# Attention stages spaced three slots apart, and one more batch by the seven-product scheme, in an attention and mixture-of-experts kernel

## The chip, the cores and the metric

The kernel runs on one core of a Trainium2 chip. The metric is the device time of one execution in microseconds (us); smaller is better. The kernel before takes 452.4 us (median of three runs, 452.1 to 457.5). The profile is of one execution; its span, from the first to the last instruction, is 450.9 us.

## What is computed

A block of cross attention between a sequence `x` (8 batches, 8 heads, 512 rows, width 64) and a small state (32 rows per head) goes in both directions; its rows then go through a top-1 mixture of eight experts.

```python
scores = x @ state.T * scale;  a  = softmax(scores);   xread = a @ state     # 512 rows per head
scores2 = state @ x.T * scale; a2 = softmax(scores2);  sread = a2 @ x        # 32 rows per head
tok = concat([xread, sread], axis=2) -> 8 * 544 tokens of width 512
e = argmax(tok @ w_gate);  gate = softmax(tok @ w_gate)[e]
out[tok] = gate * (relu(tok @ w1[e]) @ w2[e])       # w1[e]: 512 x 1024, w2[e]: 1024 x 512, float32
```

## The kernel before

The kernel treats the 512 `xread` rows of a batch as one group that goes to the expert which most of them choose (rows that choose another are handled by a branch at the end). It never forms `xread`, but multiplies the states into the expert's first matrix (`G = state @ w1`, in `states_w1`), and then works with the attention weights `a` (in the code `aT[b]`) directly. For each batch there are then two big products on the tensor engine (PE): `up`, `hT = relu(G.T @ aT)`, into PSUM tiles `ph`; and `down`, `hT.T @ w2`, into tiles `py`. The 32 state rows of each head go later through the experts in three *rounds* (tiles `pgh`, `pgy`), whose weights are loaded from DRAM again (tiles `s`).

PE works through the batches' products one after the other. All other work is cut into pieces, Python generators, that are put between the products' matmuls: each `next(insert)` is one *slot*, and emits the next pieces. Every engine works through its instructions in the order in which they were emitted, and each batch's attention passes through the slots as a pipeline of stages:

```python
def stages(b):                       # one batch's attention, before the change
    xt, sx = new_xt(), new_sx()
    turn_x(b, xt, slice(0, 4)); turn_x(b, xt, slice(4, 8))   # DVE: xt <- x_nat (two transposes)
    turn_states(b, gp.tensor_copy)                           # DVE stT, then POOL copies stT, stG
    yield
    states_gates(b)                  # PE pg <- stT;  ACT gst <- pg
    pc = new_pc()                    # the one PSUM tile of four banks for scores
    scores(b, xt, pc, 0)             # PE pc
    yield
    scores(b, xt, pc, 1)
    for i in range(4):
        turn_scores(pc, sx, i)       # DVE sx <- pc
    less_max(sx, ALL, gp)            # DVE mx <- sx, then POOL sx <- sx - mx
    yield
    exponential(sx, ALL)             # ACT sx
    soft[b] = (sx,) + write_weights(pc, write_max(pc))   # DVE nm <- pc, then ACT a <- pc, nm (reads pc)
    over_sum(sx, ALL, gp)            # DVE sm, then POOL sx <- sx * sm
    yield
    turn_read(b)                     # DVE aT <- sx, stored to at_dram by the SP queue
    yield
    yield                            # (an empty stage)
    turn_write(b)                    # PE pt <- a;  ACT a2T <- pt
    yield
    write_rows(b)                    # PE pw; ACT xs <- pw; SP stores srow, then loads x_nat, states of batch b + 3
    exps, gates = logits_x(b)        # PE pl; DVE: the top-1 choice of each row
    yield
    exps(); xsT = turn_rows(b)       # ACT; PE pxs, ACT xsT
    yield
    choose(b); logits_s(b, xsT)      # PE pr; DVE eb: the batch's expert.  PE pls; DVE lgs
    gates()

def first():                         # what is left of batches 0 and 1
    write_rows(0);  yield
    turn_write(1);  yield
    exps, gates = logits_x(1);  yield
    exps(); choose(1); e1 = expert_of(eb, 1)     # the SP queue reads the expert's number
    at_once(w1_parts(1, e1))                     # SP: four loads of w1 for batch 1
    lazy.extend(w2_parts(1, e1)); gates();  yield
    write_rows(1);  yield
    xsT = [turn_rows(b) for b in range(2)];  yield
    for b in range(2): logits_s(b, xsT[b])

def attention():
    gens, slot = [first()], 0
    while gens:
        b = 2 + slot // 4
        new = slot % 4 == 0 and b < B            # a new batch in every fourth slot
        if new:
            gens.append(early.pop() if early else stages(b))
            if b > 2: next(gens[-1])             # its first stage, ahead of the others' in this slot
        for g in gens[:len(gens) - new]: next(g)     # (ends of generators left out)
        slot += 1
        yield

def others():
    yield from attention()
    yield from sort_states()         # the state rows are sorted by expert
    change_pools()                   # attention's tiles are given up; pools for rounds and sums are opened
    yield from rounds(0, NRS)        # NRS = 3
```

The general PSUM tiles (`ph`, `py`, `pG`, `pl`, `pw`, `pt`, `pr`, `pls`, `pg`) share one pool of four banks, `ps_p`. A tile that is asked for waits until an earlier one of the four has been read.

`sort_states` is a chain of small DVE operations from one PE result (`prs`) to the slot of each row. POOL then scatters the rows to DRAM:

```python
    # pr ("prs"): counts by PE; then on DVE ng, cum, ge, eg, gates, base, rk, slot, slot_i, srow, more, own, left ...
    for t in range(NST):             # NST = 2
        gp.indirect_dma_start(out=ss_dram[:], ..., in_=srow[:, t, :])        # POOL
```

Batches below `NE` take the plain products; the others take both by halves, in seven products of half size in place of eight (Strassen's scheme), with operand sums made by DVE and POOL:

```python
def up(G, a, hT, i=ALL, insert=None, every=2, fs=range(NFC)):    # NFC = 8
    for f in fs:
        ph = bank("ph")[:, 0:128 * n]
        for g in range(2): pe.matmul(ph, lhsT=G[:, g, ts(f, 128)], rhs=a[:, i, g, :], ...)
        relu(hT[f // 2][:, f % 2]..., ph...)                     # ACT
        if insert and f % every == every - 1: next(insert, None) # four slots

def down(hT, w2t, store, insert=None, between=None):
    for c in range(NC):                                          # NC = 4
        py = bank("py")
        for f in range(NFC):
            pe.matmul(py[:], lhsT=hT[f // 2][:, f % 2, ts(c, 128)], rhs=w2t[:, f, :], ...)
            if insert and f == 3: next(insert, None)
        store(c, py)                                             # ACT y <- py, and its store
        ...  # between(c): the next batch's G at c == 1 (batch 0: c == 2); then a slot: eight slots in all

def down_by_halves(b, hT, w2t, insert, between):
    Sa, Sb, Ta, Tb = (new_sums(t) for t in ("Sa", "Sb", "Ta", "Tb"))   # in the pools of change_pools
    sums(Sa, ...)                                                # DVE, two adds
    gp.tensor_tensor(Ta[:], W(0, 1), W(0, 0), ALU.subtract)      # POOL
    sums(Sb, ...)                                                # DVE
    gp.tensor_tensor(Tb[:], W(1, 1), W(0, 1), ALU.subtract)      # POOL
    product(pX, A(0, 0), W(0, 0));  ...;  done()                 # done(): a slot; no sums needed
    product(pD, Sa, Ta);  ...;  done()
    ...                                                          # pX again, pY, pZ, pW, pD again: seven slots

def batch(b):
    if b < NE: down(hT, w2s[b], store_batch(b), slots, between)
    else:      down_by_halves(b, hT, w2s[b], slots, between_products)    # also makes the next batch's sums
    if b + 1 in sums_of: hT = up_by_halves(G, aT[b + 1], sums_of[b + 1], new_hT(), slots)   # four slots
    elif b + 1 < B:      hT = up(G, aT[b + 1], new_hT(), insert=slots)

NE = 3
aTl = const.tile([128, B - NE, 4, 2, 128], FP32)      # weights of the batches from NE on; the others' lie in attention's pool
```

`rounds` fetches ahead, and yields empty slots between its pieces:

```python
        round_in(r0); fetch(S1B - 2, S2B)
        for _ in range(4): yield
        for r in range(r0, r1):
            round_x(r); ...; yield
            for k in range(NDC):
                round_up(r, k); fetch(...); yield
                if k < NDC - 1 and r + 1 < r1: yield             # an empty slot, not in the last round
            round_relu(r); yield
            round_h(r); yield
            for f in range(0, NFC, 2):
                ...round_down(r, f + i); fetch(0, 1)...
                if f + 2 == NFC: round_out(r)
                yield
                if r + 1 < r1 or f < 4: yield
```

Of the kernel before, what the change touches and what calls it, by code (L numbers as in the profile page):

```python
# [20 lines left out]
def kernel(  # L21
# [34 lines left out]
    B, H, S, D = x.shape  # L56
# [10 lines left out]
    NDC = DM // 128  # L67
    NFC = F // 128
# [88 lines left out]

    NE = 3  # L160
    aTl = const.tile([128, B - NE, 4, 2, 128], FP32)
    aT = {b: aTl[:, b - NE] for b in range(NE, B)}

# [31 lines left out]
    G = hT = None  # L195
# [45 lines left out]
    def less_max(sx, i, eng):  # L241
        mx = att.tile([128, 4, NB], FP32, tag="mx", bufs=2, name="mx")
        dve.tensor_reduce(mx[:, i], sx[:, i], AX.X, ALU.max)
        eng.tensor_tensor(sx[:, i], sx[:, i], spread(mx, i), ALU.subtract)
# [11 lines left out]
    def write_max(pc):  # L256
        nm = att.tile([128, 2], FP32, tag="nm", bufs=2, name="nm")
        dve.tensor_reduce(nm[:], pc[:, :, 0:256].rearrange("p i (g s) -> p g i s", g=2), AX.XY, ALU.max)
        dve.tensor_scalar(nm[:], nm[:], -SCALE, None, ALU.mult)
        return nm  # L260

    def write_weights(pc, nm):

        a2 = att.tile([128, 2, NC, 128], FP32, tag="a2", name="a2")
        s2 = att.tile([128, 2], FP32, tag="s2", bufs=2, name="s2")
        for g in range(2):
            act.activation(a2[:, g].rearrange("p c (i t) -> p i c t", i=4),
                           pc[:, :, ts(g, 128)].rearrange("p i (c t) -> p i c t", c=NC),
                           AF.Exp, bias=nm[:, g:g + 1], scale=SCALE, accum_out=s2[:, g:g + 1])
        return a2, s2  # L270
# [54 lines left out]
    def logits_x(b):  # L325
        pl = bank("pl")[:, 0:128]
        for g in range(2):
            for i in range(4):
                pe.matmul(pl[ts(i, 32)], lhsT=gst[:, b, g, :], rhs=aT[b][:, i, g, :],
                          start=(g == 0), stop=(g == 1), skip_group_check=True)  # L330
        lg = att.tile([128, NC, 32], FP32, tag="lg", bufs=2, name="lg")
        dve.transpose(lg[:].rearrange("p c e -> p (c e)"), pl)
        return route(lg[:, :, 0:E], b * NC, NC)

    def stages(b):


        xt, sx = new_xt(), new_sx()
        turn_x(b, xt, slice(0, 4))
        turn_x(b, xt, slice(4, 8))  # L340
        turn_states(b, gp.tensor_copy)
        yield
        states_gates(b)
        pc = new_pc()
        scores(b, xt, pc, 0)
        yield
        scores(b, xt, pc, 1)
        for i in range(4):
            turn_scores(pc, sx, i)
        less_max(sx, ALL, gp)  # L350
        yield
        exponential(sx, ALL)
        soft[b] = (sx,) + write_weights(pc, write_max(pc))
        over_sum(sx, ALL, gp)
        yield
        turn_read(b)
        yield
        yield
        turn_write(b)
        yield  # L360
        write_rows(b)
        exps, gates = logits_x(b)
        yield
        exps()
        xsT = turn_rows(b)
        yield
        choose(b)
        logits_s(b, xsT)
        gates()

    def turn_rows(b):

        pt = bank("pxs")
        pe.transpose(pt[:, 0:128], rows_of[b][:].rearrange("p g d -> p (g d)"), ident[:])
        xsT = att.tile([128, 4, NS], FP32, tag="xsT", bufs=2, name="xsT")
        act.copy(xsT[:].rearrange("p q n -> p (q n)"), pt[:, 0:128])
        return xsT
# [208 lines left out]
    def new_hT():  # L586

        return [ffn.tile([128, 2, S], FP32, tag="hT", bufs=NFC // 2, name="hT") for _ in range(NFC // 2)]

    def up(G, a, hT, i=ALL, insert=None, every=2, fs=range(NFC)):  # L590

        n = i.stop - i.start
        for f in fs:
            ph = bank("ph")[:, 0:128 * n]
            for g in range(2):
                pe.matmul(ph, lhsT=G[:, g, ts(f, 128)], rhs=a[:, i, g, :], start=(g == 0), stop=(g == 1))
            relu(hT[f // 2][:, f % 2].rearrange("p (c i t) -> p i c t", c=NC, i=4)[:, i],
                 ph.rearrange("p (i c t) -> p i c t", i=n, c=NC))
            if insert and f % every == every - 1:
                next(insert, None)  # L600
        return hT

# [382 lines left out]
    def rounds(r0, r1):  # L985
        need1.extend((r, k, half) for r in range(r0, r1) for k in range(NDC) for half in range(2))
        need2.extend((r, f) for r in range(r0, r1) for f in range(NFC))
        round_experts(r0)
        fetch(2, 0)
        yield  # L990
        yield
        round_in(r0)
        fetch(S1B - 2, S2B)
        for _ in range(4):
            yield
        for r in range(r0, r1):
            round_x(r)
            if r + 1 < r1:
                round_experts(r + 1)
                round_in(r + 1)  # L1000
            yield
            for k in range(NDC):
                round_up(r, k)
                fetch(2, 2 if r == NRS - 1 and k > 1 else 0)
                yield
                if k < NDC - 1 and r + 1 < r1:
                    yield
            round_relu(r)
            yield
            round_h(r)  # L1010
            yield
            for f in range(0, NFC, 2):
                for i in range(2):
                    round_down(r, f + i)
                    fetch(0, 1)
                if f + 2 == NFC:
                    round_out(r)
                yield
                if r + 1 < r1 or f < 4:
                    yield  # L1020


# [3 lines left out]
    def first():  # L1026

        write_rows(0)
        yield
        turn_write(1)  # L1030
        yield
        exps, gates = logits_x(1)
        yield
        exps()
        choose(1)
        e1 = expert_of(eb, 1)
        at_once(w1_parts(1, e1))
        lazy.extend(w2_parts(1, e1))
        gates()
        yield  # L1040
        write_rows(1)
        yield
        xsT = [turn_rows(b) for b in range(2)]
        yield
        for b in range(2):
            logits_s(b, xsT[b])

    def attention():

        gens, slot = [first()], 0  # L1050
        while gens:
            b = 2 + slot // 4
            new = slot % 4 == 0 and b < B
            if new:
                gens.append(early.pop() if early else stages(b))
                if b > 2:
                    next(gens[-1])
            for g in gens[:len(gens) - new]:
                try:
                    next(g)  # L1060
                except StopIteration:
                    gens.remove(g)
            slot += 1
            yield
# [8 lines left out]
    def batch(b):  # L1073

        nonlocal G, hT

        def between(c):
            nonlocal G
            if c == (1 if b else 2) and b + 1 < B:
                G = states_w1(new_G(), w1s[b + 1], stG[:, b + 1])  # L1080
            yield
            if c == 1 and 0 < b < B - 2:
                lazy.extend(w1_parts(b + 2, expert_of(eb, b + 2)))
            yield

        def between_products(n):
            nonlocal G
            if n in (3, 4) and b + 1 < B:
                if n == 3:
                    G = new_G()  # L1090
                states_w1(G, w1s[b + 1], stG[:, b + 1], (n - 3,),
                          lambda name: late["ps_t"].tile([128, 512], FP32, tag="t", bufs=2, name=name))
            yield
            if n == 4 and b + 2 < B:
                lazy.extend(w1_parts(b + 2, expert_of(eb, b + 2)))
            if n == 5 and b + 1 < B:
                sums_of[b + 1] = up_sums(G, aT[b + 1])
            yield

        if b < NE:  # L1100
            down(hT, w2s[b], store_batch(b), slots, between)
        else:
            down_by_halves(b, hT, w2s[b], slots, between_products)
        if 0 < b < B - 2:
            lazy.extend(w2_parts(b + 2, expert_of(eb, b + 2)))
        if b + 1 in sums_of:
            hT = up_by_halves(G, aT[b + 1], sums_of[b + 1], new_hT(), slots)
        elif b + 1 < B:
            hT = up(G, aT[b + 1], new_hT(), insert=slots)
        if b == 0:  # L1110
            e2 = expert_of(eb, 2)
            lazy.extend(w1_parts(2, e2) + w2_parts(2, e2))
# [127 lines left out]
```

## Time and profile before

| | us |
|---|---|
| time, median of three | 452.4 |
| span of the profiled execution | 450.9 |
| PE busy | 438.8 |
| DVE busy | 199.3 |
| ACT busy | 125.6 |
| POOL busy | 120.3 |

The profile names the engines PE (tensor), PEld (its weight loads), DVE (vector), ACT (scalar), POOL (GpSimd) and SP (the queue that issues most loads). One float32 matmul of the code is two instructions of the trace. A line of the timeline has the start, the duration, the engine, the operation with its tiles, the number of instructions merged, and in brackets how long the engine stood idle before it and what ended the wait. A line of the chain of waits has start, duration and tile.

### The profile page before, as it was taken

To read this page: it belongs to the slowest core of one execution; us is meant where nothing else is said; L and a number is where in the kernel's file an instruction comes from. 1 tells how busy PE (TensorE), PEld (TensorE's weight loads), DVE (VectorE), ACT (ScalarE), POOL (GpSimd) and SP (SyncE) were. 2 spreads that over 40 slices of the span, in tenths; PEclk is the share of its full clock that TensorE was granted. 3 is DMA by queue.
4 is the path that set the end of the run, shared out by engine and by line. 5 is a ranking of instruction groups with operands and counts; after the bars stand their busy time and mean duration, and the time that the engine had idled before them with its cause. 6 is when DMAs were issued, how large, how long until landed. Compare 5 with 4: busy or idle time off the path is not lost.

```text
span 450.9 us, 9945 instructions
## 1 busy us (share of the span) xinstructions
PE 438.8 (97%) x3861; PEld 276.8 (61%) x3861; DVE 199.3 (44%) x452; ACT 125.6 (28%) x283; POOL 120.3 (27%) x108
## 2 busy tenths in 40 slices
PE   8899999999999999999999999999999999999995
PEld 7675545455455455444757776776667776657673
DVE  4758771757383753142241441445143433326142
ACT  1543243434242442313210332024111312024100
POOL 2010140314121211006233413542253423532220
PEclk9999999999999999999999999999999999999998
DMA  6990399324858443519999999799969997498301
GB/s 189 328 312 6 109 322 298 129 87 125 302 146 307 134 161 117 171 49 292 391 383 321 391 388 331 276 354 388 346 217 337 367 405 252 156 365 307 115 26 59
DMA packets 68418, 110.04 MB, mean 244 GB/s; under 512 B 12943, under 2 KB 27279, under 8 KB 68368
## 3 DMA queue, kind: packets, MB, share of 16 engines
q1 hardware_dynamic: 60240, 99.99, 64.2%
q10 hardware_dynamic: 7728, 8.34, 5.2%
q0 software_dynamic: 400, 1.05, 0.6%
q8 instruction: 31, 0.51, 0.5%
q14 instruction: 19, 0.16, 0.1%
HBM read 94.15 MB, written 14.95 MB: 242 GB/s over the span
## 4 chain that ended last, share of the span: by engine, by line
PE 86%; DVE 9%; DMA 2%; issue 1%; POOL 1%; ACT 1%; SPq 0%; POOLq 0%; DVEq 0%
PE ph L48 19%; PE py L48 14%; PE pD L48 8%; PE pX L48 8%; PE pgh L48 5%; PE pgy L48 5%; PE pY L48 4%; PE pW L48 4%; PE pZ L48 4%; PE pc L48 4%; PE pG L48 3%; DVE xt L48 3%; DVE sm L48 2%; PE pw L48 2%; PE pt L48 2%; DMA w1t<-in_moe_w_dram 2%
## 5 line engine op out<-in xcount | busy, mean ns | idle before, releaser
L48 PE MATMUL py<-w2t,hT 128*128 128x512 f32 x192 | 87.6, 601 | 0.0
L48 PEld LDWEIGHTS py<-w2t,hT 128*128 128x128 f32 x192 | 34.6, 190 | 38.7 <-issue 38.0
L48 POOL TENSOR_TENSOR Ta<-w2t,Ta 128x1024 f32<-128x1024 f32 x10 | 26.2, 2621 | 74.5 <-PE pD L48 44.9
L48 PE MATMUL ph<-aTe,G 128*128 128x128 f32 (+2 forms) x160 | 44.9, 430 | 1.2 <-DVE aTe L48 1.1
L48 DVE TENSOR_TENSOR hT<-ph,hT 128x512 f32<-128x512 f32 x40 | 27.7, 692 | 37.4 <-PE ph L48 37.4
L48 ACT ACTIVATE hT<-ph 128x512 f32<-128x512 f32 (+2 forms) x56 | 26.2, 476 | 47.6 <-PE ph L48 47.6
L48 PE MATMUL pX<-w2t,hT 128*128 128x256 f32 x160 | 36.2, 379 | 0.0
L48 PEld LDWEIGHTS ph<-aTe,G 128*128 128x128 f32 x160 | 24.6, 190 | 16.7 <-issue 12.3
L48 PEld LDWEIGHTS pX<-w2t,hT 128*128 128x128 f32 x160 | 30.2, 190 | 4.4 <-issue 0.5
L48 PE MATMUL ph<-aTl,G 128*128 128x256 f32 (+1 forms) x96 | 29.6, 456 | 0.0
L48 POOL TENSOR_TENSOR sx<-sx,mx 128x1024 f32<-128x1024 f32 x6 | 11.5, 1912 | 60.8 <-DVE mx L48 60.8
L48 DVE SCALAR_TENSOR_TENSOR yh<-pY,gw,yh 128x256 f32<-128x256 f32 x20 | 8.3, 476 | 39.6 <-PE pY L48 39.6
L48 PEld LDWEIGHTS ph<-aTl,G 128*128 128x128 f32 x96 | 17.7, 190 | 12.7 <-issue 11.4
L48 ACT ACTIVATE yh<-pX,gw 128x256 f32<-128x256 f32 x30 | 12.0, 473 | 44.8 <-PE pX L48 44.8
L48 ACT COPY G<-pG 128x512 f32<-128x512 f32 x32 | 16.9, 593 | 26.3 <-PE pG L48 26.3
L48 PE MATMUL pgh<-s,sxT 128*32 128x512 f32 x192 | 24.0, 598 | 0.0
L48 PE MATMUL pgy<-s,shT 128*32 128x512 f32 x192 | 23.4, 598 | 0.0
L48 DVE STREAM_TRANSPOSE sx<-pc 128x256 f32<-128x256 f32 x32 | 11.7, 418 | 23.4 <-PE pc L48 23.4
L48 ACT ACTIVATE hT<-hT 128x512 f32<-128x512 f32 x24 | 14.8, 631 | 23.7 <-DVE hT L48 23.7
L48 ACT ACTIVATE y<-py,gw 128x512 f32<-128x512 f32 x12 | 8.2, 687 | 44.1 <-PE py L48 44.1
L48 POOL TENSOR_TENSOR sx<-sx,sm 128x1024 f32<-128x1024 f32 x6 | 11.5, 1914 | 30.7 <-ACT xsT L48 17.0
L48 PE MATMUL pG<-w1t,stG 64*32 64x512 f32 x256 | 18.3, 599 | 0.5 <-DMA w1t<-in_moe_w_dram 0.5
(175 smaller groups left out, 654.8 us busy)
## 6 DMA issues: line engine op xcount, KB each, us to landing
s<-in_moe_w_dram SPq DMA_DIRECT2D x192, 256.0 KB, 5.3
w2t<-in_moe_w_dram SPq DMA_DIRECT2D x32, 512.0 KB, 6.7
w1t<-in_moe_w_dram SPq DMA_DIRECT2D x28, 512.0 KB, 6.0
x_nat<-in_x_dram SPq DMA_DIRECT2D x16, 512.0 KB, 5.4
out_dram<-yh ACTq DMA_DIRECT2D x19, 256.0 KB, 4.9
out_dram<-y ACTq DMA_DIRECT2D x12, 256.0 KB, 2.8
at_dram<-aTl SPq DMA_DIRECT2D x5, 512.0 KB, 5.0
w1t<-in_moe_w_dram SPq DMA_DIRECT2D x2, 1024.0 KB, 7.2
```

The costliest lines, as they stand in the source:

```text
L48: ins = getattr(self.engine, name)(*args, **kw)
```

## The change

Attention is to be over sooner, so that the pools of the seven-product scheme are open one batch earlier. A new batch enters in every third slot instead of every fourth; the stages of a batch go from ten to nine, as one empty stage is dropped; the writing half's maximum and exponentials (`write_max`, `write_weights`) move one stage earlier, next to the scores that they read; `first()` writes batch 1's rows two stages earlier. `up` for batch 2 gives six slots instead of four, so that attention, the sort and the change of pools fit in before batch 2's second product. That product, and batch 3's first, then go by halves (`NE = 2`). The rounds have seven more slots to fill and spread their pieces over them.

```diff
-    NE = 3
+    NE = 2
@@ def stages(b)
     less_max(sx, ALL, gp)
+    soft[b] = (sx,) + write_weights(pc, write_max(pc))
     yield
     exponential(sx, ALL)
-    soft[b] = (sx,) + write_weights(pc, write_max(pc))
     over_sum(sx, ALL, gp)
     yield
     turn_read(b)
-    yield
     yield
     turn_write(b)
@@ def up
-def up(G, a, hT, i=ALL, insert=None, every=2, fs=range(NFC)):
+def up(G, a, hT, i=ALL, insert=None, at=(1, 3, 5, 7), fs=range(NFC)):
-            if insert and f % every == every - 1:
+            if insert and f in at:
@@ def rounds
-        for _ in range(4):
+        for _ in range(7):
             yield
-                if k < NDC - 1 and r + 1 < r1:
+                if k < NDC - 1:
                     yield
-                if r + 1 < r1 or f < 4:
+                if r + 1 < r1 or f + 2 < NFC:
                     yield
@@ def first
     exps, gates = logits_x(1)
+    write_rows(1)
     yield
     (exps, choose(1), the loads of w1 for batch 1)
     gates()
     yield
-    write_rows(1)
-    yield
     xsT = [turn_rows(b) for b in range(2)]
+    yield
     yield
@@ def attention
-            b = 2 + slot // 4
-            new = slot % 4 == 0 and b < B
+            b = 2 + slot // 3
+            new = slot % 3 == 0 and b < B
@@ def batch
-            hT = up(G, aT[b + 1], new_hT(), insert=slots)
+            hT = up(G, aT[b + 1], new_hT(), insert=slots, at=(1, 3, 5, 7) if b + 1 < NE else (1, 3, 4, 5, 6, 7))
+            assert b + 1 < NE or "sst" in late
```

## The prediction

> **What bounds the kernel now.** I read the page first, then busy time by windows of 15 us, then PE's waits, the chain of waits, and the timeline of two stretches. The page:
>
> ```profile
> PE 438.8 (97%) x3861; PEld 276.8 (61%) x3861; DVE 199.3 (44%) x452; ACT 125.6 (28%) x283; POOL 120.3 (27%) x108
> PEclk9999999999999999999999999999999999999998
> ```
>
> PE is the bound, at full clock. A change helps if it takes matmul time away, or one of the few waits, and brings no new wait of PE. The windows (columns: PE, PEld, DVE, ACT, POOL busy, clock, DMA share, GB/s):
>
> ```profile
> 90.00:105.00 15.00, 14.57 (x266) 8.26 (x265) 7.29 (x25) 5.65 (x12) 3.21 (x5) 1.00 0.23 72
> ...
> 210.00:225.00 15.00, 15.00 (x79) 10.85 (x77) 3.97 (x6) 4.62 (x10) 3.38 (x2) 1.00 1.04 380
> ```
>
> In attention PE loses 0.43 us of 15; after it (from 210 us) nothing shows, though DMA is full there. PE's waits say what the 0.43 is (total, times, longest):
>
> ```profile
> PE pg L48 <- POOL stT L48: 2.1, 5, 0.4
> ...
> PE pG L48 <- DMA w1t<-in_moe_w_dram: 0.5, 2, 0.3
> ```
>
> The chain of waits, where it runs through PE, gives the length of each product:
>
> ```profile
> 192.22 7.06 PE py L48 x16
> 199.40 13.84 PE ph L48 x32
> 213.23 3.45 PE pX L48 x16
> 216.69 3.45 PE pD L48 x16
> ...
> 246.04 7.11 PE ph L48 x32
> ...
> 255.00 5.38 PE ph L48 x24
> ...
> 404.45 2.75 PE pgh L48 x16
> ```
>
> At 199.40 stands batch 3's plain up, at 213.23 the start of its down by halves, at 246.04 and 255.00 an up by halves. The pgh of 2.75 us takes 1.85 elsewhere: there it waits for a round's weights.
>
> [...] (below, Ta starts 0.02 us after the scatter ahead of it on POOL, its own data long there). [...] here a subtract of 1024 elements took 2.41 us on POOL (Ta) and 1.22 on DVE (sx). [...] In the trace before, PE's waits hold 0.5 us in all that are put down to ACT (pg after G), so the banks rotate well; the change alters that.
>
> **What the change takes away.**
> - Batch 2's down: eight pieces of 8 matmuls, from the chain 3.63 + 3.44 + 3.63 + 3.44 + 3.63 + 3.43 + 7.06 = 28.3 us. By halves, batch 3's from 213.23 on: 3.45 + 3.45 + 3.46 + 3.65 + 3.65 + 3.65 + 3.45 = 24.8. Gain 3.5.
> - Batch 3's up: 13.84 becomes 7.11 + 5.38 = 12.5. Gain 1.35.
> - The waits of pg: before, DVE does a batch's nm and sm ahead of the next batch's xt and stT. Now xt follows nm directly; from the end of the scores, sx, mx, nm, xt, stT and POOL's copy take 1.5 + 1.2 + 1.4 + 2.3 + 0.7 + 0.7 = 7.8 us, and PE comes to pg after two products and 1.6 us of small matmuls, some 8.8. Gain 2.1.
> - The waits for round weights, 0.9 at 404 and 0.36 at one pgy (2.21 against 1.85): the same loads over 62 slots instead of 55. Gain 1.2.
>
> Sum: 8.2 us. The rest of attention's matmuls (some 5.3 us a batch) is only moved.
>
> **What it adds.** I followed the built program of the changed kernel, which shows each engine's order and for which instruction each wait stands, and laid durations of this trace on it.
>
> (1) The sums behind the sort. Before, batch 3's plain up lay between the sort and the first sums:
>
> ```profile
> 199.21 0.19 PE L48 MATMUL prs<-oh,ones_b 128*128 128x8 bf16 x2
> ...
> 199.43 0.17 DVE L48 TENSOR_SCALAR ng_i<-prs 128x8 int32<-128x8 f32 x1 [5.10 <-PE prs L48]
> ...
> 203.29 1.17 POOL L48 DMA_INDIRECT ss_dram<-srow,slot_i  x1 [30.94 <-DVE more L48]
> 204.76 0.97 POOL L48 DMA_INDIRECT ss_dram<-srow,slot_i  x1 [0.30 <-PE ph L48]
> 205.75 2.41 POOL L48 TENSOR_TENSOR Ta<-w2t 128x1024 f32<-128x1024 f32 x1
> ```
>
> From prs to Ta's end are 208.2 - 199.4 = 8.8 us: 3.9 of small DVE operations, 2.4 of scatters, 2.4 of subtract. Before, 13.8 us of ph and pX hid them. Now prs is followed by pX alone (3.45 us), and pD needs Ta. The scatters stand ahead of Ta on POOL. PE waits 8.8 - 3.5 = 5.3 us.
>
> (2) PSUM banks behind ACT. This stretch shows the length of the path from scores to exponentials:
>
> ```profile
> 97.38 1.07 PE L48 MATMUL pc<-xt,stT 32*32 32x128 f32 x64
> 98.49 1.44 DVE L48 STREAM_TRANSPOSE sx<-pc 128x256 f32<-128x256 f32 x4 [4.84 <-PE pc L48]
> 99.97 1.22 DVE L48 TENSOR_REDUCE mx<-sx 128x32 f32<-128x1024 f32 x1
> ...
> 104.97 1.22 DVE L48 TENSOR_REDUCE nm<-pc 128x2 f32<-128x1024 f32 x1
> ...
> 106.42 0.69 ACT L48 ACTIVATE a<-pc,nm 128x512 f32<-128x512 f32 x1 [1.73 <-DVE nm L48]
> ```
>
> With nm moved up, the scores' end is followed by sx 1.5, mx 1.2, nm 1.4 and the two exponentials 1.5: ACT is free again 5.7 us later. The exponentials now stand in ACT's queue ahead of what empties banks in the next slot, and PE gets there after 3.6 us (a piece of product). Three places ask for a bank that ACT empties behind them. In slot 6, pl needs pw's bank, emptied by xs (0.55): 5.7 + 0.55 against 5.1 (piece, pls, pw), about 1.3 us. In batch 1's up, ph of f = 4 needs that of f = 2, emptied by a relu (0.6): 6.3 against 5.0, 1.3 us. In batch 2's G, the last pG needs the bank of a py, emptied by y (0.7): 6.4 against 4.6, 1.8 us. Sum 4.4.
>
> (3) The first G. Batch 1's expert must be known before its w1 is loaded. DVE now does batch 3's xt and stT (3.0 us) ahead of that choice, and the SP queue issues batch 1's rows and batch 4's input ahead of the load. Choice: from the scores' end at 55.2 (in the timeline 54.15, and 1.0 for pw, now ahead of them), 1.5 + 1.2 + 1.4 + 2.3 + 0.7 + 0.8 = 63.1, before 58.7. So the load starts 4.4 us later, and PE reaches that G 1.7 us later (pw earlier, and pxs, pg and pc in place of pw). It waited about 0.5 already. Some 2.7 us more are lost; part of it falls on a wait of pg for the same choice (its bank is pr's).
>
> Sum: 5.3 + 4.4 + 2.7 = 12.4 us. In the other slots of the three-slot cycle (some 16 us of PE, 11.5 of DVE) I find no wait over 0.2 us. The end of the last batch stands as before: round 2's last pgy stays one slot ahead of the last pD.
>
> Total: 452.4 - 8.2 + 12.4 = 456.6, say 456.5.
>
> **Rivals.** (R1) The products are all that counts: PE is 97% busy, so 4.9 us go and the new waits lie beside other work; with pg's waits, 445.5. For it: DVE, ACT and POOL are under half busy. Against it: a share over the span says nothing of prs to Ta, a chain of three engines with 3.5 us of PE work beside it. (R2) DVE becomes the bound of the three-slot cycle: 11.5 us of work plus its waits for POOL and ACT fill 16 us, each cycle stretches by 1 us or more, and the time passes 461. For it: aT waits for POOL's multiply and stands ahead of the next sx. Against it: by my sum aT ends 0.5 us before the next slot's choice, and 2.5 before sx. (R3) DMA: the inputs come in three quarters of the time. Against it: the window at 90 us moves 72 GB/s, that at 210 us 380. It would cost something only at the first G.
>
> **Range and chances.** The gain in products is sure to 0.5 us. Wait (1) rests on a chain that I saw whole; it may be 4.5 to 6. Those of (2) and (3), 7.1 us together, rest on sums of four to six terms, and each could vanish or double: 3 to 10. So 451 to 461. Faster by over 2% needs under 443.4, less than R1 gives: 0.03. Slower by over 2% needs over 461.4, R2 or all waits large: 0.10. Within 2%: 0.87.
>
> **What would show it.** Step by step: pD of batch 2 waits some 5 us, by the profile for POOL's Ta; the waits of pg for stT are gone; pl, ph and pG wait for ACT (xs, hT, y) 1 to 2 us each; the first pG waits for w1t some 3 us; down of batch 2 has 24.8 us of PE work and up of batch 3 has 12.5; DMA share falls in the rounds. It is wrong if pD starts right behind pX, if DVE is over 80% busy in the cycle, or if PE waits in every cycle.

## The result, and the profile after

The changed kernel takes 466.8 us (median of six runs, 465.6 to 468.0), the kernel before 452.55 beside it: a ratio of 1.030, 95% interval 1.025 to 1.034. The change makes the kernel slower by 14 us. The prediction was 456.5, with 451 to 461 as its range.

The page of the changed kernel: busy time by engine, the granted clock in forty slices, and the shares of the chain of waits.

```profile
PE 439.7 (95%) x3933; PEld 290.4 (62%) x3933; DVE 229.9 (49%) x482; ACT 127.0 (27%) x287; POOL 137.5 (30%) x120
PEclk9999999999999999799999999999999999999999
PE 76%; DMA 11%; DVE 8%; ACT 2%; SPq 1%; issue 1%; ACTq 0%; POOL 0%; DVEq 0%
```

PE is busy as long as before (439.7 against 438.8 us) in a span 13.8 us longer, although five microseconds of products are gone: either it works slower somewhere or "busy" hides waits. Both are true. One slice, the seventeenth, has a clock of 0.7, and DMA has 11% of the chain, where before it had 2%. PE's waits in the changed kernel (total, times, longest):

```profile
PE pD L48 <- DMA s<-in_moe_w_dram: 5.7, 1, 5.7
PE pG L48 <- DMA w1t<-in_moe_w_dram: 5.3, 6, 1.9
PE ph L48 <- ACT hT L48: 1.7, 1, 1.7
PE pl L48 <- ACT xs L48: 1.7, 1, 1.7
...
PE pg L48 <- DVE c_cc L48: 0.6, 1, 0.6
PE pg L48 <- POOL stG L48: 0.5, 1, 0.5
PE pg L48 <- POOL stT L48: 0.4, 1, 0.4
```

Batch 2's pD waits once, 5.7 us. The name behind it, a load of s, only happens to be the last event; the next view shows what it waits for. The five waits of pg for stT are one of 0.4, and two new ones stand beside it.

The timeline of batch 2's first products in the changed kernel, PE, POOL and DVE:

```profile
180.07 3.70 PE L48 MATMUL pX<-w2t,hT 128*128 128x256 f32 x16
189.47 5.52 PE L48 MATMUL pD<-Ta,Sa 128*128 128x256 f32 x16 [5.69 <-DMA s<-in_moe_w_dram]
...
184.11 1.17 POOL L48 DMA_INDIRECT ss_dram<-srow,slot_i  x1 [18.88 <-DVE more L48]
185.59 1.45 POOL L48 DMA_INDIRECT ss_dram<-srow,slot_i  x1 [0.30 <-ACT yh L48]
187.06 2.36 POOL L48 TENSOR_TENSOR Ta<-w2t 128x1024 f32<-128x1024 f32 x1
...
186.71 6.16 DVE L48 TENSOR_TENSOR Sb<-hT 128x512 f32<-128x512 f32 x2
```

Ta ends at 189.42 and pD starts at 189.47: it waits for Ta, behind two scatters, as predicted. But this pD takes 5.52 us, where the pX before it takes 3.70 with as many matmuls. The windows (clock is the third figure from the end) say why:

```profile
186.00:188.00 2.00, 0.00 (x0) 0.00 (x0) 2.00 (x3) 0.00 (x0) 1.99 (x2) 0.58 0.90 225
190.00:192.00 2.00, 2.00 (x6) 1.59 (x5) 2.00 (x1) 0.00 (x0) 1.71 (x1) 0.50 1.03 397
```

The clock fell to a half in the idle time and stayed there until about 193 us (0.71 from 192 to 194). A wait of 5.7 us cost 7.6.

At the first G (batch 1's) the changed kernel shows this, PE first, then the SP queue:

```profile
64.13 3.70 PE L48 MATMUL py<-w2t,hT 128*128 128x512 f32 x8
69.77 2.14 PE L48 MATMUL pG<-w1t,stG 64*32 64x512 f32 x8 [1.94 <-DMA w1t<-in_moe_w_dram]
72.11 1.05 PE L48 MATMUL pG<-w1t,stG 64*32 64x512 f32 x4 [0.20 <-DMA w1t<-in_moe_w_dram]
74.14 1.91 PE L48 MATMUL pG<-w1t,stG 64*32 64x512 f32 x20 [0.99 <-DMA w1t<-in_moe_w_dram]
...
63.45 3.52 SPq L48 DMA_DIRECT2D w1t<-in_moe_w_dram  x4
```

The same in the kernel before:

```profile
66.07 1.37 PE L48 MATMUL pG<-w1t,stG 64*32 64x512 f32 x12
67.70 1.91 PE L48 MATMUL pG<-w1t,stG 64*32 64x512 f32 x20 [0.26 <-DMA w1t<-in_moe_w_dram]
...
59.20 1.98 SPq L48 DMA_DIRECT2D w1t<-in_moe_w_dram  x4
```

w1 comes in four parts, four pG for each part in either half of G. Four pG alone take 1.05 us (at 72.11), but sixteen together take 1.09 (elsewhere in this kernel), where the page's mean of one is 0.6: they run side by side. So parts that come one by one cost PE time that shows as busy: the eight at 69.77 are two parts, one after the other. From the end of py (67.76) to the end of G (75.98) are 8.2 us, before 3.5 (66.07 to 69.54). w1 is asked for at 63.45, 4.25 us later than before (59.20), as predicted; but the four issues then take 3.52 us instead of 1.98, and the last part is there at 74.10 instead of 67.66, 6.4 us later. The chain of waits says what the fourth issue waited for:

```profile
60.83 5.79 DMA out_dram<-y
66.62 0.02 issue
66.63 7.47 DMA w1t<-in_moe_w_dram
```

In the trace every transfer of the SP and ACT queues raises one of eight semaphores (counters) as it lands; they take the eight in turn, 47 transfers each in the changed kernel. Five of the eight have all their landings on record there, and none of the 230 issues that follow another transfer on these five starts before that one has landed. The fourth part of w1, issued at 66.63, has the semaphore of a store of y from ACT's queue, which landed at 66.62. This is how the program is built, not a limit that a run here shows of the chip.

Batch 2's G suffers in the same way. Before, it took 2.0 us (first line); in the changed kernel it takes 6.7, from 134.38 to 141.12. The chain of waits of the changed kernel stands below:

```profile
122.07 2.08 PE L48 MATMUL pG<-w1t,stG 64*32 64x512 f32 x32
...
134.38 2.17 PE L48 MATMUL pG<-w1t,stG 64*32 64x512 f32 x8
138.03 1.05 PE L48 MATMUL pG<-w1t,stG 64*32 64x512 f32 x4 [1.47 <-DMA w1t<-in_moe_w_dram]
139.28 1.91 PE L48 MATMUL pG<-w1t,stG 64*32 64x512 f32 x20 [0.20 <-DMA w1t<-in_moe_w_dram]
...
124.26 7.78 DMA x_nat<-in_x_dram
132.04 0.02 issue
132.06 7.18 DMA w1t<-in_moe_w_dram
```

The last part of w1 is issued when a load of x_nat has landed, 7.78 us after its issue, and is there at 139.24. The copy y on ACT, which the prediction had as the last to be ready, ends at 137.69.

### The profile page after: what moved, and what is told of

It reads as the page before. It is cut to its first block, busy times and chain, and to the rows that moved or that the text cites. A ratio compares the mean times of both kernels' runs of the same rounds, so it can differ in the third digit from the quotient of the medians.

```text
span 464.7 us, 10165 instructions
## 1 busy us (share of the span) xinstructions
PE 439.7 (95%) x3933; PEld 290.4 (62%) x3933; DVE 229.9 (49%) x482; ACT 127.0 (27%) x287; POOL 137.5 (30%) x120
## 3 DMA queue, kind: packets, MB, share of 16 engines
q0 software_dynamic: 400, 1.05, 0.6%
## 4 chain that ended last, share of the span: by engine, by line
PE 76%; DMA 11%; DVE 8%; ACT 2%; SPq 1%; issue 1%; ACTq 0%; POOL 0%; DVEq 0%
PE ph L48 20%; PE pD L48 9%; PE pX L48 7%; PE py L48 6%; PE pgy L48 5%; PE pZ L48 5%; PE pY L48 5%; PE pW L48 5%; PE pgh L48 4%; DMA s<-in_moe_w_dram 3%; DMA w1t<-in_moe_w_dram 3%; PE pG L48 3%; PE pc L48 3%; DVE nm L48 2%; DVE sx L48 2%; DMA x_nat<-in_x_dram 2%
## 5 line engine op out<-in xcount | busy, mean ns | idle before, releaser
L48 PE MATMUL py<-w2t,hT 128*128 128x512 f32 x128 | 59.0, 604 | 0.0
L48 DVE TENSOR_TENSOR hT<-ph,hT 128x512 f32<-128x512 f32 x50 | 34.6, 692 | 40.4 <-PE ph L48 40.4
L48 PE MATMUL pX<-w2t,hT 128*128 128x256 f32 x192 | 43.8, 381 | 0.0
L48 PEld LDWEIGHTS pX<-w2t,hT 128*128 128x128 f32 x192 | 36.1, 190 | 7.3 <-issue 1.7
L48 PEld LDWEIGHTS py<-w2t,hT 128*128 128x128 f32 x128 | 23.0, 189 | 25.7 <-issue 25.1
L48 PE MATMUL ph<-aTe,G 128*128 128x128 f32 (+2 forms) x128 | 30.4, 388 | 2.7 <-ACT hT L48 1.7
L48 PE MATMUL pD<-Ta,Sa 128*128 128x256 f32 x96 | 24.0, 407 | 5.7 <-DMA s<-in_moe_w_dram 5.7
L48 PEld LDWEIGHTS pD<-Ta,Sa 128*128 128x128 f32 x96 | 19.1, 204 | 11.5 <-POOL Ta L48 6.1
L48 PEld LDWEIGHTS ph<-aTe,G 128*128 128x128 f32 x128 | 18.8, 191 | 11.6 <-issue 6.5
L48 PE MATMUL pZ<-Tb,Sb 128*128 128x256 f32 x96 | 22.3, 386 | 0.0
```

Of the source, the lines that this page charges most:

```text
L48: ins = getattr(self.engine, name)(*args, **kw)
```

## Experiments

Each starts from the changed kernel (466.8 us) unless it says otherwise. In profiles of kernels that are the same up to the first G, PE comes to that G between 67.8 and 70.4 us, and is through with it between 74.9 and 76.6, so small effects there are judged by what an instruction waited for. "The interval" is the 95% interval of a run's ratio to the kernel before; for the changed kernel it is 1.025 to 1.034.

### The wait at batch 2's first pD

**Scatters alone out of the way.**

```diff
-        for t in range(NST): scatter(t)          # in sort_states
+        for t in range(NST): late["scatter"](t)  # in rounds, one slot later
```

> Only the two scatters are emitted one slot later, behind Ta and Tb on POOL; the sort's small DVE operations stay ahead of Sa. If the scatters on POOL are the whole of the wait, Ta ends by 183 and pD waits under 1 us: time down by 6 us or more. If, as I now think, the DVE chain is the second line (Sa ends at 186.8 in the changed kernel, 3.2 us after pX), pD still waits about 3.2 us, behind DVE's Sa, and the time falls by about 2.5 to 4 us, to 463 to 464.5, with a part of the clock's loss still there.

Measured: 467.9 us, no gain. pD waits 6.85 us and then takes 6.73. DVE and POOL in that kernel:

```profile
181.94 2.34 POOL L48 TENSOR_TENSOR Ta<-w2t 128x1024 f32<-128x1024 f32 x1 [17.18 <-DVE gw L48]
184.24 2.34 POOL L48 TENSOR_TENSOR Tb<-w2t 128x1024 f32<-128x1024 f32 x1
...
182.04 2.26 DVE L48 TENSOR_TENSOR base<-cum,ng 128x8 f32<-128x8 f32 x1
184.34 2.27 DVE L48 TENSOR_SCALAR base<-base 128x8 f32<-128x8 f32 x1
...
189.25 1.29 DVE L48 TENSOR_TENSOR Sa<-hT 128x512 f32<-128x512 f32 x2 [0.21 <-DMA s<-in_moe_w_dram]
```

Ta is early now, but two operations of the sort on eight elements, 0.15 and 0.17 us in the changed kernel, each last as long as the POOL operation beside them (2.26 and 2.27 us against 2.34), and Sa stands behind them. The same shows above in Sb, 6.16 us for two adds that take 1.29 alone. POOL's Ta takes 2.34 us here and 2.36 in the changed kernel, so here only DVE's operations lengthen; why they do, no run shows. Both my expectations fall: the sort as a whole is in the way, and with the scatters out of POOL's way its subtracts run beside the sort and lengthen it.

**The sort six slots later.**

```diff
         exps()
+        gates(); change_pools()
+        for _ in range(6): yield
         pr = bank("prs")...          # the sort's chain
...
-        for _ in range(7): yield     # in rounds, between round_in and round_x
+        for _ in range(1): yield
```

> The sort's chain (PE prs, the small DVE operations, both scatters) is emitted six slots later, behind batch 2's sums and products, and the rounds have six empty slots fewer at their head, so that the rest keeps its place. Theory 1 (PE waited 5.7 us for Ta because Sa on DVE and Ta on POOL stood behind the sort, and the pD behind it then ran at half clock and lost 1.9 us more): the 5.7 us wait at batch 2's pD goes, that pD takes about 3.6 us instead of 5.5, and the time falls by 6.5 to 7.6 us, to about 459.5 to 460. Rival (the sums wait for w2 or for attention's tiles to be given up, whatever the sort does): pD of batch 2 still waits 4 us or more, and the time stays within 2 us of the changed kernel's 466.8. A second rival (the delay is only moved into the rounds, whose weights and rows come later): the wait goes, but pgh and pgy then wait 5 us or more, and the time stays.

Measured: 478.4 us. pD's wait falls to 0.7 and 1.6 us, but the second rival is right, and more strongly than it said: from the row load to its use one slot is left.

```profile
PE ptx L48 <- DMA xg<-ss_dram: 8.8, 1, 8.8
```

**Four slots later, with the first sums on DVE.**

```diff
+        for _ in range(4): yield     # as above; then round_in one slot, round_x five slots behind
+        eng = dve if b == NE else gp
-        gp.tensor_tensor(Ta[:], W(0, 1), W(0, 0), ALU.subtract)
+        eng.tensor_tensor(Ta[:], W(0, 1), W(0, 0), ALU.subtract)    # and Tb
```

> The sort's chain and scatters are emitted four slots later (behind batch 2's third sums), with five slots left between them and the first row load's use, and batch 2's four first sums Sa, Ta, Sb, Tb all run on DVE, so that POOL and DVE do not work beside each other there. By the two runs before, the wait at batch 2's first pD is made of three things: the sort ahead of the sums, DVE and POOL slowing each other, and the clock that falls in the idle time. Theory: with all three taken away pD waits under 1 us and takes about 3.6 us, and the time falls by 6 to 7 us, to about 460 to 461. Rival (the sort is needed where it is, since the rounds' rows come late when it moves): pD no longer waits, but ptx waits for xg or pgh for s by 4 us or more, and the time stays above 464.

Measured: 474.0 us. The first pD waits 0.8 and takes 3.69: theory right. The rounds give it back: pgh waits 3.0 us for s, batch 2's last pD 1.5 for yh, which stands behind the sort on DVE. One pgh, whose weights come part by part, takes 9.6 us with its waits, where the others take 1.9:

```profile
242.55 5.57 PE L48 MATMUL pgh<-s,sxT 128*32 128x512 f32 x14 [1.78 <-DMA s<-in_moe_w_dram]
```

The rival holds: the sort cannot go far.

**One slot later.** Sa and Ta first, then the sort, then Sb and Tb, all on DVE for batch 2; six empty slots instead of seven.

```diff
+        for _ in range(1): yield
...
+        eng = dve if b == NE else gp             # Ta, its second difference, Tb
+        if b > NE: second_sums()                 # Sb, Tb; for batch 2 behind the sort's slot
```

> The sort's chain is emitted one slot later only (five of the six head slots of the rounds' wait stay), so that batch 2's Sa and Ta stand ahead of it; batch 2's Sa, Ta, second Ta, Sb and Tb all run on DVE, Sb and Tb behind the chain, and the scatters have POOL to themselves. The moves by four and six slots took the wait at pD away but gave it back in the rounds, whose weights were asked for later. Theory: with one slot only the rounds do not notice, pD waits under 1 us and takes 3.6 us, and the time falls by 5.5 to 7 us, to 460 to 461.3. Rival (the rounds' weights are so tight that one slot, 3.6 us, already costs as much): pD no longer waits, but pgh and pgy take 4 us or more longer in all, and the time stays above 464.

Measured: 460.2 us (ratio to before 1.015, 1.012 to 1.019), 6.6 us less than the changed kernel. In the profile 8.0 us pass from batch 2's first pX to its second instead of 14.8, of which pD waits 0.7 (for ACT's yh). This settles the wait: 5.7 us of waiting and 1.9 of lowered clock, most of which can be had back. From the second pX to the end 2.0 us are lost again, 1.3 of them in a new wait of ph for hT; pgh and pgy show no wait for s.

**The clock alone.** Idle matmuls, whose result nobody reads, fill the wait; first 22, then 11.

```diff
+        for _ in range(22):      # then 11; batch 2 only
+            pe.matmul(idle[:, 0:256], lhsT=ident[:], rhs=W(0, 0)[:, 0], ...)
         pD = new_bank("pD")
```

> 22 matmuls whose result nobody reads (256 columns each, some 0.216 us, 4.75 us in all) are put between batch 2's pX and its first pD, into the 5.7 us in which PE only waits; nothing else changes. If the idle time is what lowers TensorE's clock (0.50 at 188 to 192 us in the changed kernel), the clock stays near 1.0 in that stretch, pD takes about 3.6 us instead of 5.5, and the time falls by about 1.9 us although PE does more work. If the clock falls for another reason, pD stays at about 5.5 us and the time stays or rises.

Measured: 467.65 us. The trace counts a float32 matmul as two (44 instructions here), so the 22 ran 9.66 us and overran the wait; pD behind them took 3.62.

> As the run with 22 idle matmuls between pX and pD, but with 11: a float32 matmul stands as two in the trace, so those 22 took 9.7 us instead of 4.75 and overran the wait of 5.7. 11 take 4.8 us. If the idle time lowers the clock, pD takes 3.6 to 3.8 us instead of 5.5 and the time falls by 1.5 to 1.9 us, to 465. If not, pD stays at 5.5 and the time at 466.8.

Measured: 464.8 us, 2.0 less for more work (interval 1.022 to 1.029, which overlaps that of the changed kernel; the clock is the clearer evidence). The timeline of this kernel and one window of it:

```profile
182.37 4.91 PE L48 MATMUL idle<-w2t,ident 128*128 128x256 f32 x22
188.22 3.72 PE L48 MATMUL pD<-Ta,Sa 128*128 128x256 f32 x16 [0.95 <-POOL Ta L48]
```

```profile
190.00:192.00 2.00, 2.00 (x12) 1.74 (x11) 2.00 (x3) 0.00 (x0) 0.47 (x1) 1.00 0.88 337
```

With the idle time filled, the clock from 190 to 192 us is 1.00 instead of 0.50 and pD takes 3.72 us instead of 5.52: here it was the idle time that lowered the clock. In this profile the wait is also named as what it is, POOL's Ta.

### The waits behind ACT's exponentials

```diff
         scores(b, xt, pc, 1)
+        nm = write_max(pc)
         for i in range(4): turn_scores(pc, sx, i)
         less_max(sx, ALL, gp)
-        soft[b] = (sx,) + write_weights(pc, write_max(pc))
+        soft[b] = (sx,) + write_weights(pc, nm)
```

> In each batch's scores stage DVE does nm (the largest of pc) ahead of the transposes sx and of mx, instead of behind them. The exponentials of a then start about 2.7 us earlier, and nm's second operation no longer runs beside POOL's subtract. Theory (ACT's exponentials stand in front of xs and the relu that empty PE's banks): both waits of 1.7 us, of pl for xs and of ph for hT, fall below 0.3 us, and the time falls by 3 to 3.5 us, to 463.5. Rival (the banks wait for something else, or sx, now 1.4 us later, brings a new wait of the same size through POOL and aT): the waits stay or others of 1 to 2 us come in their place, and the time stays within 1 us of 466.8.

Measured: 461.3 us, 5.5 less (interval 1.014 to 1.025), more than the 3 to 3.5 expected. pl's wait for xs falls from 1.7 to 0.6, ph's for hT goes, and batch 2's G takes 4.8 us instead of 6.7 (a y stood behind the exponentials there). nm's second operation takes 0.17 us again; in the changed kernel it took 0.85 to 0.92 beside POOL's subtract, the same lengthening as above, which made the exponentials later than my sum. From one batch's pr to the next's, the three-slot cycle takes 16.1 us in this kernel, and no PE wait shows in two of these cycles, though DVE is 78 to 79% busy in them. In the changed kernel, which gives DVE the same operations in another order, the cycle with ph's wait takes 17.9.

### The first G

**Batch 1's write_rows back.**

```diff
         exps, gates = logits_x(1)
-        write_rows(1)
...
         gates()
         yield
+        write_rows(1)
+        yield
         xsT = [turn_rows(b) for b in range(2)]
-        yield
```

> Batch 1's write_rows (PE pw, ACT xs, and the SP queue's stores of rows and loads of batch 4's x and states) goes back to where it stood before the change, behind the loads of batch 1's w1. Theory 2 (the first pG waits because the issues of w1 stand behind batch 4's loads on the SP queue, and their completion is held up by older transfers): the four w1 issues follow each other within about 0.5 us instead of 3.5, the wait of the first pG for w1t falls by 2 to 4 us, and the time by 2 to 4 us, to 463 to 465. Rival (the choice behind DVE's xt and stT is all of it, the loads start as late as before): the wait at the first pG stays above 4 us, and the time stays within 1 us of 466.8, or rises by a wait of batch 4's xt for its later x.

Measured: 466.4 us. The issues still take 3.05 us, now because the third itself takes 1.40 (an issue of w1 takes 0.33 to 0.37 before); the store of y is no longer in the way of the fourth. The last w1 is there at 72.11, 2.0 us earlier than in the changed kernel, without a gain in time that shows. So the loads in front are not all that spreads the issues.

**The choice ahead of batch 3's first stage.**

```diff
+                if b == 3: next(gens[0])       # first(): choose(1)
                 if b > 2: next(gens[-1])
-            for g in gens[:len(gens) - new]:
+            for g in gens[1 if slot == 3 else 0:len(gens) - new]:    # first() not twice in this slot
```

> In the slot in which batch 1's expert is chosen, that choice is emitted ahead of batch 3's first stage, so that on DVE xt and stT (3.0 us) stand behind it. Theory (the choice's place on DVE sets when w1 can be asked for): eb is ready some 3 us earlier, the w1 issues start at about 60.5 instead of 63.45, and the waits at the first pG, 3.1 us in the list plus what its slow groups hide, fall by 2.5 to 3 us; pg then waits up to 1 us more for stT, which is later. Net 1.5 to 3 us less, 464 to 465.3. Rival (the issues are held by older transfers, batch 4's x and the stores of y, whatever the choice does): the issues start earlier but are spread over 5 us or more, and the last part of w1 lands no earlier than 73.

Measured: 466.65 us. The first G then runs without a wait, in 1.95 us, but pg waits 3.8 us for stT, far more than the 1 us I allowed, and the py behind it takes 5.28 us instead of 3.70.

**Both.**

> Of the first combination only two edits: batch 1's write_rows back in its place and the choice ahead of batch 3's first stage; all else as in the changed kernel. Each alone moved the time by less than 0.5 us. Theory A (two things in series hold w1: the choice, and batch 4's loads in front of it; either alone leaves the other): together they bring the first G 2.5 to 3.5 us earlier and the time to 463.3 to 464.3. Theory B (what held the first G in the single runs was nm's and the exponentials' place, as part of the choice's way on DVE): together they bring under 1 us, and the time stays at 466.

Measured: 467.25 us. Theory A fails on the time, but the profile shows why:

```profile
60.17 1.98 SPq L48 DMA_DIRECT2D w1t<-in_moe_w_dram  x4
...
61.91 0.19 DVE L48 TENSOR_REDUCE gw<-r_ex 128x4 f32<-128x32 f32 x1 [2.26 <-ACT r_ex L48]
62.43 2.34 DVE L48 STREAM_TRANSPOSE xt<-x_nat 128x1024 f32<-128x1024 f32 x2
...
65.41 0.23 PE L48 MATMUL pg<-wg,stT 64*32 64x8 f32 x2 [3.26 <-DVE stT L48]
```

w1 is asked for 3.3 us earlier and in 1.98 us. But batch 1's gates stand between the choice and xt on DVE, and need r_ex from ACT, which stands behind the exponentials (59.15 to 60.5) and a y. DVE idles 2.26 us, and PE then 3.3 at pg; py behind it ran at a clock of 0.52.

**The gates one slot later as well.**

```diff
-        gates()
         yield
+        gates()
```

> The run with batch 1's write_rows back and the choice ahead of batch 3's first stage, with one edit more: batch 1's gates, three small DVE operations that need ACT's r_ex, come one slot later. In that run w1's issues began 3.3 us earlier and took 2.0 us instead of 3.5, but DVE stood for 2.26 us at those gates, because r_ex on ACT stands behind the exponentials of a and a y, and xt and stT stood behind the gates: pg waited 3.3 us. Theory (this wait is what ate the gain): pg's wait for stT falls below 1 us, the first G ends 2 to 2.5 us earlier than in that run, and the time is 464 to 465. Rival (w1 lands no earlier than 71 to 72 us in any case): pG then waits for w1t 2 us or more, and the time stays at 466.5.

Measured: 465.0 us. pg's wait for stT falls from 3.3 to 0.4, as the theory says, and the median is 2.2 us below that of the run before (their intervals, 1.021 to 1.028 and 1.026 to 1.035, just overlap). pG still waits 0.8 for w1. In this profile part is lost again later: after the 1.7 us wait of pl the clock fell to 0.50, and a py took 5.03 us instead of 3.70.

**The stores of aT one stage later.**

```diff
-        if i.stop == 4: sp.dma_start(out=at_dram[b], ...)     # in turn_read; stays for batches 0 and 1
+        keep_read(b)                                          # the same, ahead of write_rows(b)
```

> Only the stores of aT to DRAM (batches from 2 on) are issued one stage later, so that on the SP queue the w1 loads of the next batch do not stand behind a store that waits for DVE. Theory: the last two parts of batch 2's w1 are issued about 2 us earlier, batch 2's G no longer loses 1.7 us to w1t, though the y behind it may still cost 0.6 to 1; the time falls by 0.7 to 1.7 us, to 465.1 to 466.1. Rival (DMA is busy there and the loads land no earlier): no change, 466.8.

Measured: 465.7 us. The interval (1.024 to 1.031) overlaps that of the changed kernel, and batch 2's G takes 6.5 us instead of 6.7: a gain is not shown.

### The parts, and versions together

**The products undone.** `NE = 3` again, all else as changed.

> The part on the products is undone alone: batch 2's down and batch 3's up are plain again (NE = 3), the three-slot cadence and the rounds' empty slots stay. By the prediction's sum this takes back 4.9 us of gain and, since batch 3's plain up lies between the sort and the first sums again, the wait of 5.7 us and the slow pD behind it (1.9 us): net 2.7 us less than the changed kernel, 464. If the loss is only moved (the rounds bear it), it stays at 466 or more; if the two new products were a true gain of 4.9 us, it rises to 471.

Measured: 463.6 us against 464 expected. The four times lie between 461.4 and 466.5, and the interval (1.016 to 1.029) overlaps that of the changed kernel, so the run bears out the direction, not the 2.7 us. The two terms are read from the changed kernel's own profile: batch 2's down has 24.9 us of PE work and batch 3's up 12.3, where the plain ones had 28.3 and 13.8 (4.9 us gained), and the wait and the slow pD cost 7.6.

**First combination.** The sort four slots later with batch 2's first sums on DVE, and the edits of write_rows, choice, nm and aT's stores.

> All of it together: sort later and batch 2's first sums on DVE, batch 1's write_rows back in its place, the choice ahead of batch 3's first stage, nm first, and the stores of aT to DRAM one stage later, so that the w1 loads of batch 2 do not stand behind them. If the waits are separate and add up: 6.5 at pD, 3.5 at the first G, 3.4 at pl and ph, 1.5 at batch 2's G, 15 us in all, about 452, level with the kernel before. If one wait only shows another behind it, the sum is missed by 4 us or more, and the time stays above 456.

Measured: 463.9 us. Batch 2's first pX starts 9.8 us earlier than in the changed kernel, and the rounds take most of that back (pgh waits 2.9 us for s).

**Second.** The same with the sort one slot later.

> The sums ahead of the sort by one slot, together with the four changes of attention's part that the combination before had (batch 1's write_rows back, the choice ahead of batch 3's first stage, nm first, aT's stores later). That combination came to batch 2's first product 9.8 us earlier than the changed kernel and gave 5 to 12 us back in the rounds. If the rounds' loss came from the sort's four slots, this one keeps the 9.8 us and adds the 6 of pD's wait: 450 to 452, level with or just faster than the kernel before. If DMA has to move the same weights in a time that attention no longer fills, whatever the sort does, the rounds wait 3 us or more for s again and the time is 455 to 460.

Measured: 453.4 us, ratio to before 0.999 (0.997 to 1.002): level. The parts alone had moved the time by -6.6 (sums first), -5.5 (nm first), -1.1 (aT's stores) and +0.4 us (rows and choice), which would give 454.0: the waits are separate and add up. Of what is left, this kernel's SP and ACT queues and PE show one piece:

```profile
186.98 16.01 SPq L48 DMA_DIRECT2D s<-in_moe_w_dram  x20
...
195.55 7.41 ACTq L48 DMA_DIRECT2D out_dram<-yh  x3
...
203.64 1.99 PE L48 MATMUL ph<-aTl,G 128*128 128x256 f32 x8 [2.16 <-ACT hT L48]
```

ACT stands 7.4 us at three stores, each of which takes 0.4 us to issue, and the copy of hT behind them makes PE wait. The stores share the eight semaphores with SP's loads: the second is issued at 198.69, just after a load of s with its semaphore landed (198.62).

**Third.** Twelve of the twenty loads spread over three slots.

```diff
-        fetch(S1B - 2, S2B)
-        for _ in range(6): yield
+        fetch(S1B - 2, 0)
+        for i in range(6):
+            yield
+            fetch(0, 1 if i < S2B else 0)
```

> The second combination, and the rounds' first three weight tiles (twelve of twenty loads that the SP queue issued in one go) spread over three slots. In that combination ACT's queue stood for 7.4 us at three stores of yh, while SP issued twenty loads in 16 us, and PE waited 2.2 us for hT behind them. Theory (the stores wait for the burst): ACT's stores take under 3 us, the wait for hT goes, and the time falls by 2 us, to about 451.5, below the kernel before. Rival (DMA is full there in any case): the wait stays or moves to s, and the time stays at 453.4.

Measured: 451.5 us (ratio 0.996, 0.994 to 0.998, which touches the interval of the second). The wait for hT falls from 2.2 to 0.2, but 1.5 of this is that PE comes to that ph 1.5 us later in this profile (a py further up took 5.40 us); the ph starts 0.45 us earlier. ACT's stores still take 6.15 us, and all three are issued 0.07 to 0.08 us after a load of s with their semaphore has landed. So the theory is right about what the stores wait for, and spreading the loads hardly changed it.

**Fourth.** With the gates one slot later.

> The third combination (spread loads) with the same edit. There DVE stood 1.0 us at the gates and pg waited 1.3 us for stT, and pG 0.6 for w1t behind it. If DVE is the last to be ready, 1 us is gained, to 450.5; if w1t is, 0.3 or nothing, 451.2 to 451.5.

Measured: 450.5 us, ratio to before 0.995 (0.993 to 0.997): the lowest median, and 16 us below the changed kernel. It is 2 us, or half a per cent, below the kernel before; that it is faster than the third is not shown, as their intervals overlap. pg no longer waits for DVE's stT; pG waits 1.5 us in all for w1, and ph 0.8 for hT.

## Why the prediction was wrong, by its steps

- **Products (4.9 us gained).** Right: 24.9 and 12.3 us of PE work in the profile, against 24.8 and 12.5 predicted.
- **Waits of pg (2.1).** Mostly right: 2.1 became 0.4, gain 1.7.
- **Round weights (1.2).** The slow pgh of 2.75 us is gone, but nothing is left of it: pth now waits 1.0 (for ACT's G), and two pgy take 2.1 and 2.25 us, where before one took 2.21. From batch 3's first pX to the end it took 237.7 us before; after, it takes 235.4, and 2.3 of the rounds' work (a ptx and a pgh) is done ahead of it: 237.7 again.
- **(1) The sums behind the sort (5.3).** The mechanism and the wait were right, 5.7; the step left out what an idle PE costs next: 1.9 us at half clock, 0.50 after the wait of 5.7 us. Cost 7.6.
- **(2) Banks behind the exponentials (4.4).** Right in place for pl and ph, but too small: 1.7 each against 1.3 (for pl its own terms, 5.7 + 0.55 - 5.1, give 1.15). It had nm's second operation at 0.17 us, and beside POOL it takes 0.85. Batch 2's G is the larger miss: 6.7 us where it took 2.0 before, 4.7 more against 1.8. The step let it end with y; y is there at 137.7 and the last part of w1 at 139.24, and parts that come one by one cost PE time by themselves. nm first took 1.9 of it. Cost 8.1.
- **(3) The first G (2.7).** The failed step, and the same assumption failed at batch 2's G. "The load starts 4.4 us later, and PE reaches that G 1.7 us later" was true (4.25 and 1.7), and the difference was taken for the loss, which supposes that the load takes as long as before. It took 10.7 us from first issue to last landing instead of 8.5. In the prediction's terms, the path to that G does not end with the choice: the fourth issue stands behind the landing of a store of y (5.8 us), which the step does not have. G's stretch grew by 4.7 us, and pg waits 1.1 more: 5.8.

By these the changed kernel's profile would be 14.9 us longer than the one before (-4.9 - 1.7 + 7.6 + 8.1 + 5.8). Its start ran 1.4 us faster (the py at 53.78 us stands at 54.15 before, and pw, 1.0 us, is already done), which leaves 13.5; measured are 13.8 (464.7 against 450.9). So (3) is the least certain: in eight other profiles of kernels that are the same up to there, the first G's stretch takes 5.7 to 7.9 us instead of 8.2, the less the later PE comes to it. Of the prediction's miss of 10 us, 3.7 are (2), nearly all of it w1 of batch 2, 3.1 are (3), 2.3 are (1), and 1.6 gains that did not come, with the 1.4 of the start against them. That all four went one way is no accident: each was a chain laid on the old trace's durations, and in the old trace the four issues of w1 take 1.98 us and PE's longest wait is 1.5, where the new order has 3.52 and 5.7. That DVE slows beside POOL did stand in it: an add Sa at 232.24 us takes 1.41 us beside POOL's Ta, the next one 0.68.

The rivals: R1, that only the products count, falls with the result. For R2, DVE is 49% busy over the span, but 74 to 81% in the three cycles from 81 to 135 us; that it is still not the bound is shown by the run with nm first, where the cycle takes 16.1 us with the same work on DVE. R3, DMA, which I allowed "only at the first G", mattered there, at batch 2's G and in every attempt to move the rounds. No run took the store of y alone out of the way of w1, so its share of the loss at the first G is read from the trace, not tried.

## What to carry to other kernels

When an order of instructions is changed, follow every late transfer to its landing, not to its issue, ask what the issue itself waits for, and follow every longer wait of PE to the clock behind it. An operation moved off one engine's queue may lengthen another's, as 0.15 us on DVE became 2.26 beside POOL: look for the two running beside each other. And a load that is needed late may still have to be asked for early: here four slots' delay of the sort cost more than the wait it removed.

## What the hardware showed unexpectedly

DVE operations of 0.15 to 0.2 us took 0.85 to 2.27 beside a POOL tensor operation, even on two elements a partition. The clock fell after short waits too: to 0.50 after pl's wait of 1.7 us in the run with the gates later, but not after the same wait in the changed kernel, where the py behind it took its 3.70; to 0.50 after waits of 1.3 and 0.5 us in the third combination, but not in the second, which has the same two waits; and not at the first G of the changed kernel, where the windows show 1.00. What decides it was not found.
